# Softcap attention and a maxout MoE block on one core: the fourth quad's softmax sums from VectorE additions and four products

## The chip, the cores and the metric

One core of a Trainium2 chip runs the whole program. The metric is the device time of one execution in microseconds, as the median of several executions. A profile belongs to one execution of its own; its span leaves out a little at the start and the end.

A core has five engines that run at the same time, each through its own list of instructions: TensorE (PE; its weight loads are PEld), VectorE (DVE), ScalarE (ACT), GpSimd (POOL) and SyncE (SP, which here only issues DMAs). An engine works through its list in order; it waits where an instruction needs what another engine or a DMA has not delivered yet.

## The reference

Attention with a soft cap on the scores, and then a block with two input matrices whose larger result is taken:

```python
scores = (q @ k.T) / sqrt(64)                  # 8 batches, 12 heads, 448 x 448
scores = cap * tanh(scores / cap)              # cap = 30
attn   = exp(scores - max(scores))
attn   = attn / (sum(attn, axis=-1) + 1e-9)
x      = (attn @ v)                            # 3584 tokens x 768
g      = maximum(x @ w1, x @ w2)               # 3584 x 1024
out    = g @ w_out                             # 3584 x 768
```

What matters here is the sum over the keys, one number for each query of each head.

## The kernel before

Heads are taken in pairs: eight batches of six pairs give 48 pairs, and two neighbouring pairs make a *quad*, so there are 24 quads, t = 0 to 23. Three pairs make a *group* for loading (g = 0 to 15).

The scores are computed transposed: keys on partitions, queries along the row. A head's 448 keys are three chunks of 128 (j = 0 to 2) and a rest of 64. `scores(t, p)` forms the products of pair p of quad t (p = 2 holds the rests of both pairs), and ScalarE takes the tanh out of PSUM at once (L319). `ex` then takes the exponential (L324) into the tiles `expo[t, 0]`, `expo[t, 1]` and `expo[t, 2]`, in bfloat16. No maximum is subtracted.

Since keys lie on partitions, their sum is a product with a matrix of ones. `total(t)` (L352) does it for the four heads of a quad in four column strips of 32, in one PSUM bank. It has two forms. For t < NS it takes each chunk by itself: three chunks and the rest for four heads, sixteen products (L358, L362). For other quads VectorE has added the chunks elementwise beforehand into the tile `esum[t]`, and `total` needs one product for each head, four in all (L365). The additions are made by `add(t, ab, step)` (L331), which returns at once for t < NS: step 0 adds chunks 0 and 1 of pair ab (L344), step 1 adds chunk 2 (L346), step 2 adds the rest, which fills 64 partitions (L342). Two pairs and three steps make six additions for a quad.

After the sums, VectorE turns them (L367), takes reciprocals (L369) and turns them back (L371); `values(t)` forms the products with v (L381, L387), and `normalize` multiplies (L402), which writes x.

The MoE block of a batch, `moe(b)`, needs x of three quads. Its work is *fill*: a generator whose single products are handed out by `F(n)`, so many between other instructions. Its first layer makes eight groups of six products (L414) of x with `wd_sb`, which holds the difference of the two input matrices; each group is emptied from PSUM by VectorE with a relu (L419). Then come the output products (L429 with x, L432 with g), emptied by L435. The PSUM banks for all of these, `mm`, come from a pool of two, so a group can start only when the group two before it has been emptied.

The order of everything is written out by hand. There is a prologue for quads 0 to 2, and a loop over t from 3 to 23, in which the scores of quad t+1 are formed while the sums and values of quad t are finished. In the loop the calls of `add` for quad t are strewn between fills: after 6 and 2 products `add(t,0,0)`, after 3 more `add(t,0,1)`, after 3 `add(t,1,0)`, then 2, the scores of the next quad, 3, `add(t,1,1)`, 7, `add(t,0,2)`, 4, `add(t,1,2)`, 8, the rest scores, `total(t)` and `values(t)`. In the turn t = 3 one subtraction for the weights, `subtract(5, 1, nc.vector)` (L236), stands ahead of `add(t,0,1)`.

Keys and queries of groups from 2 on are loaded in float32 by SP, cast to bfloat16 by GpSimd (L185, L190, L197) into `kqf`, and transposed by a DMA that SP issues (`cross`, L292) into `qkT`, from which the scores are formed. Values are cast by GpSimd too (L164, L169). During the turn t = 3 GpSimd makes the last subtraction of the weights that falls to it, casts keys and queries of the end of group 3, and then casts values.

Of the kernel before, what the change touches and what calls it, by code (L numbers as in the profile page):

```python
# [10 lines left out]
def kernel(  # L11
# [287 lines left out]
    def two_banks(pool):  # L299
        return pool.tile([P, 2, 512], f32, name="s" if pool is s_psum else "v")  # L300
# [30 lines left out]
    def add(t, ab, step):  # L331

        if t < NS or t >= NQ:
            return
# [17 lines left out]
    def total(t):  # L352

        ss = two_banks(s_psum)[:, 0, :]
        if t < NS:
            for j in range(NJ):
# [117 lines left out]


    NL = N // L
    NS = 4
    todo = [[] for _ in range(N)]
    crosses = {}
    casts = [[] for _ in range(NQ)]  # L480
# [247 lines left out]
```

## Time and profile before

| quantity | value |
|---|---|
| median of 5 executions | 340.42 us (339.79 to 341.38) |
| the profiled execution | 340.82 us, of which its span is 338.8 us |
| granted TensorE clock | 1.00 |
| sixteen products of a sum (L358, L362), quad 3 | start 63.02 us, next work starts 63.78 us |
| four products of a sum (L365), quad 4 | start 75.22 us, next work starts 75.42 us |
| an addition into esum (L344, L346, L342) | 0.61 us at the least, 0.96 and 1.45 at the most for L344 and L346 |
| eviction of a group of the first layer (L419) | 0.62 us |
| DMA bytes moved | 61.78 MB, mean 182 GB/s |

Times in the profile count from the start of the span. A line of an order of time gives the start, the length, the engine, the line of the kernel, the operation, what it writes and reads with the shapes, how many such instructions are merged, and in brackets the idle time before it with what ended it.

### The profile page before, as it was taken

The page shows a single profiled execution, that of the slowest core. Times are in us where ns is not written, and L with a number is a line of the kernel's source. Part 1 is how long each engine was busy: PE and PEld are TensorE (multiplying, and loading weights), DVE is VectorE, ACT ScalarE, POOL GpSimd, SP SyncE. Part 2 cuts the span into 40 slices and gives each one's busy share as a digit, 9 for nine tenths or more (in the row PEclk, how much of TensorE's full clock was granted, in tenths as well). Part 3 has the DMA queues.
Part 4 walks back from the last instruction along what each step waited for, and adds up shares of the span by engine and source line. Part 5 has one row for each costly group of instructions (what it writes and reads, how often), then busy time and mean ns, then how long its engine had stood idle before and what let it go on. Part 6 is the DMA issues. An engine that isn't in the chain of part 4 may idle for free.

```text
span 338.8 us, 6879 instructions
## 1 busy us (share of the span) xinstructions
PE 324.5 (96%) x2722; PEld 163.7 (48%) x2722; DVE 229.7 (68%) x414; ACT 278.5 (82%) x243; POOL 112.6 (33%) x196
## 2 busy tenths in 40 slices
PE   3799999999899999999999999999999999999995
PEld 2455544455345454455445544545444554555562
DVE  4546866687787776767777668775876777874421
ACT  4999989999999999899989999999989999800000
POOL 8335687554224422431440442144034220000000
PEclk9999999999999999999999999999999999999999
DMA  7999999999996699558958599749955920012032
GB/s 218 192 234 268 275 261 273 268 240 259 206 301 148 186 228 269 143 141 206 303 124 198 75 250 316 170 121 236 304 104 133 221 94 2 0 48 93 2 93 93
DMA packets 106239, 61.78 MB, mean 182 GB/s; under 512 B 62816, under 2 KB 101216, under 8 KB 106208
## 3 DMA queue, kind: packets, MB, share of 16 engines
q1 hardware_dynamic: 102336, 58.21, 67.2%
q0 software_dynamic: 3872, 3.15, 6.0%
q8 instruction: 21, 0.34, 0.5%
q14 instruction: 10, 0.08, 0.1%
HBM read 42.47 MB, written 11.01 MB: 158 GB/s over the span
## 4 chain that ended last, share of the span: by engine, by line
PE 80%; DMA 9%; POOL 4%; DVE 4%; SPq 1%; issue 1%; POOLq 0%; DVEq 0%
PE mm L432 22%; PE mm L414 18%; PE mm L429 16%; PE v L381 6%; PE s L318 6%; DMA gT<-in_moe_w_dram 3%; PE mm L256 2%; PE v L318 2%; DMA osb<-in_moe_w_dram 2%; PE s L315 2%; PE v L387 2%; PE s L365 2%; DMA qkT<-kqf 2%; POOL wd_sb L236 2%; DMA vr<-in_v_dram 1%
## 5 line engine op out<-in xcount | busy, mean ns | idle before, releaser
L324 ACT ACTIVATE expo<-tanh 128x2688 bf16<-128x2688 bf16 (+1 forms) x72 | 140.3, 1950 | 0.2
L319 ACT ACTIVATE tanh<-s 128x896 bf16<-128x896 f32 x123 | 107.5, 915 | 14.1 <-PE s L318 10.6
L432 PE MATMUL mm<-wo_sb,gT 128*128 128x384 bf16 x448 | 85.8, 327 | 0.0
L414 PE MATMUL mm<-xT,wd_sb 128*128 128x448 bf16 x384 | 78.1, 353 | 0.9 <-DVE gT L419 0.7
L429 PE MATMUL mm<-wm_sb,xT 128*128 128x384 bf16 x336 | 66.1, 327 | 0.0
L435 DVE COPY osb<-mm 128x384 f32<-128x384 f32 x56 | 31.1, 556 | 44.5 <-PE mm L432 44.0
L432 PEld LDWEIGHTS <-gT 128*128 128x128 bf16 x448 | 42.3, 98 | 34.4 <-issue 8.2
L414 PEld LDWEIGHTS <-wd_sb 128*128 128x128 bf16 x384 | 35.9, 98 | 39.1 <-issue 8.5
L419 DVE TENSOR_SCALAR gT<-mm 128x448 bf16<-128x448 f32 x64 | 39.5, 622 | 19.8 <-PE mm L414 19.6
L688 POOL COPY mark<-inv 1x1 f32<-1x1 f32 x17 | 3.0, 178 | 125.3 <-DVE inv L371 109.7
L429 PEld LDWEIGHTS <-xT 128*128 128x128 bf16 x336 | 31.6, 98 | 26.4 <-issue 6.7
L319 ACT ACTIVATE tanh<-v 128x896 bf16<-128x896 f32 x45 | 41.5, 923 | 0.0
L381 PE MATMUL v<-expo,vp 128*32 128x448 bf16 x576 | 36.0, 353 | 0.0
L318 PE MATMUL s<-qkT 64*128 64x448 bf16 x198 | 28.5, 363 | 1.9 <-DVE qkT L288 1.5
L402 DVE TENSOR_TENSOR xT<-v,inv 128x448 bf16<-128x448 f32 x48 | 27.7, 620 | 2.6 <-PE v L387 0.3
L346 DVE TENSOR_TENSOR esum<-esum,expo 128x896 bf16<-128x896 bf16 x40 | 27.4, 686 | 0.8
L367 DVE STREAM_TRANSPOSE st<-s 128x448 f32<-128x448 f32 x24 | 15.6, 650 | 17.0 <-PE s L365 12.7
L344 DVE TENSOR_TENSOR esum<-expo 128x896 bf16<-128x896 bf16 x40 | 26.6, 666 | 0.0
L342 DVE TENSOR_TENSOR esum<-esum,expo 64x896 bf16<-64x896 bf16 x40 | 24.7, 617 | 1.2
L318 PEld LDWEIGHTS <-qkT 64*128 64x128 bf16 x288 | 10.5, 95 | 24.4 <-issue 16.9
L381 PEld LDWEIGHTS <-vp 128*32 128x32 bf16 x576 | 15.6, 97 | 10.2 <-DVE vl L161 0.4
L185 POOL CAST kqf<-qr 128x1152 bf16<-128x1152 f32 (+2 forms) x17 | 17.1, 1003 | 7.4 <-DMA qr<-in_q_dram 6.5
(68 smaller groups left out, 265.5 us busy)
## 6 DMA issues: line engine op xcount, KB each, us to landing
vr<-in_v_dram SPq DMA_DIRECT2D x14, 576.0 KB, 5.0
out_dram<-osb SPq DMA_DIRECT2D x20, 384.0 KB, 3.6
kr<-in_k_dram SPq DMA_DIRECT2D x12, 576.0 KB, 6.7
qr<-in_q_dram SPq DMA_DIRECT2D x12, 576.0 KB, 7.1
out_dram<-osb SPq DMA_DIRECT2D x16, 192.0 KB, 4.3
osb<-in_moe_w_dram SPq DMA_DIRECT2D x8, 256.0 KB, 4.8
gT<-in_moe_w_dram POOLq DMA_DIRECT2D x12, 128.0 KB, 9.4
wo_sb<-in_moe_w_out_dram POOLq DMA_DIRECT2D x4, 384.0 KB, 9.2
```

Of the source, the lines that this page charges most:

```text
L318: nc.tensor.matmul(s[:, m, :S], k0[r, j * P : (j + 1) * P], qTn[r, :])
L319: nc.scalar.activation(tanh[t, p][:, 2 * j : 2 * j + 2, :], s[:, :, :S], AF.Tanh, scale=scale / cap)
L324: nc.scalar.activation(expo[t, p], tanh[t, p][:, 0:n, :], AF.Exp, scale=float(cap))
L344: nc.vector.tensor_add(d, e_of(t, ab, 0), e_of(t, ab, 1))
L346: nc.vector.tensor_add(d, d, e_of(t, ab, 2))
L381: nc.tensor.matmul(ps[r, :S], vp[g % 2][:, 2 * n + h, j, u::2], e_of(t, ab, j)[:, h, :], start=(j == 0), stop=False,)
L402: nc.vector.tensor_mul(x_of(t, u), ps[:, u, :S], inv[t])
L414: nc.tensor.matmul(ps[:, :S], wd_sb[:, c, f * P : (f + 1) * P], x[:, c, cs], start=(c == 0), stop=(c == KC - 1))
L419: nc.vector.tensor_relu(g[f // FH][:, f % FH, cs], ps[:, :S])
L429: nc.tensor.matmul(ps[:, : DM // 2], x[:, c, ts], wm_sb[:, c, hs], start=(c == 0), stop=False)
L432: nc.tensor.matmul(ps[:, : DM // 2], g[f // FH][:, f % FH, ts], wo_sb[:, f, hs], start=False, stop=(f == FC - 1))
L435: nc.vector.tensor_copy(osb[:, hs], ps[:, : DM // 2])
```

## The change

One constant changes. `NS` is read in `add` and in `total` and nowhere else, so quad 3, the first of the loop, moves from the first form of the sum to the second: its six calls of `add` now issue additions, and its `total` issues four products from `esum[3]` instead of sixteen from the `expo` tiles. Quads 0 to 2 keep the sixteen products; quads 4 to 23 had the additions already.

```diff
     NL = N // L
-    NS = 4
+    NS = 3
     todo = [[] for _ in range(N)]
```

The lines that read it, in `add` (L333) and in `total` (L355):

```python
        if t < NS or t >= NQ:
            return
...
        if t < NS:
            for j in range(NJ):
...
        else:
            for ab, h, r in HEADS:
                nc.tensor.matmul(ss[r, :S], ones[:, :32], esum[t][:, 2 * ab + h, :], start=True, stop=True)
```

## The prediction

> **What bounds the kernel now.** I read the page's busy shares first, then the chain of waits, then the order of time around the one place that the change can touch. NS is read only in `add` (L333) and `total` (L355), so going from 4 to 3 alters quad t=3 and nothing else. Which products are t=3's? There are 48 on L358, twelve for each of four quads, and the last twelve start at 63.02 us; so the place is the loop's first turn, about 53.5 to 67 us.
>
> ```profile
> PE 324.5 (96%) x2722; PEld 163.7 (48%) x2722; DVE 229.7 (68%) x414; ACT 278.5 (82%) x243; POOL 112.6 (33%) x196
> ...
> PE 80%; DMA 9%; POOL 4%; DVE 4%; SPq 1%; issue 1%; POOLq 0%; DVEq 0%
> ```
>
> TensorE is the bound: it carries 80% of the chain, and it works through its list in a fixed order. A stall that it takes in the middle isn't won back, because no later part of it waits for slack. From 54.9 to 66.0 us (table of stages) PE is busy 10.85 of 11.10 us, ACT 11.01, POOL 8.48, DVE 7.22. VectorE seems to have 3.9 us free. The question is whether that free time lies where the additions land. TensorE in order of time (start, length, engine, line, what it writes and reads, how many):
>
> ```profile
> 57.28 0.55 PE L318 MATMUL s<-qkT 64*128 64x448 bf16 x4
> 58.07 0.36 PE L318 MATMUL v<-qkT 64*128 64x448 bf16 x2 [0.25 <-ACT tanh L319]
> 58.37 4.34 PE L414 MATMUL mm<-xT,wd_sb 128*128 128x448 bf16 x22
> 62.54 0.54 PE L315 MATMUL s<-qkT 128*128 128x448 bf16 x2
> 63.02 0.75 PE L358 MATMUL s<-expo,ones 128*32 128x448 bf16 x12
> 63.59 0.36 PE L362 MATMUL s<-expo,ones 128*32 128x448 bf16 x4
> 63.78 0.74 PE L381 MATMUL v<-expo,vp 128*32 128x448 bf16 x12
> ```
>
> Ahead of these stand 16 more products of L414, from 54.14. They and the 22 are fill, the first layer of the first MoE block: groups of six into one PSUM bank, two banks in turn (the pool `mm` has two). So group n+2 may start only when VectorE has emptied group n (L419). VectorE, GpSimd and SP's queue in the same stretch:
>
> ```profile
> 55.87 0.62 DVE L419 TENSOR_SCALAR gT<-mm 128x448 bf16<-128x448 f32 x1 [0.51 <-PE mm L414]
> 56.41 1.37 DVE L236 TENSOR_TENSOR wd_sb<-xT,gT 128x512 bf16<-128x512 f32 x1
> 57.70 0.61 DVE L419 TENSOR_SCALAR gT<-mm 128x448 bf16<-128x448 f32 x1
> ```
> ```profile
> 58.05 0.82 POOL L185 CAST kqf<-kr 128x768 bf16<-128x768 f32 x1 [0.82 <-DMA kr<-in_k_dram]
> 58.82 0.64 POOL L197 CAST kqf<-kr 64x128 bf16<-64x128 f32 x2
> 59.52 0.83 POOL L185 CAST kqf<-qr 128x768 bf16<-128x768 f32 x1
> 60.42 0.40 POOL L190 CAST kqf<-qr 64x256 bf16<-64x256 f32 x1
> ```
> ```profile
> 60.84 3.02 SPq L292 DMA_TRANSPOSE qkT<-kqf  x1
> ```
>
> See three things: the subtraction of L236 took 1.37 us on DVE while GpSimd ran its own from 56.08 to 57.23 (the other two on DVE took 0.76 and 0.68); GpSimd is casting from 58.05 to 60.82; and the moment its last cast ends, 60.82, SP issues the transposing DMA at 60.84. That one lands for the scores at 67.11, where the chain has a DMA piece of 6.22 us.
>
> **What the Trainium skill says.** "SBUF — State Buffer", section "SBUF: two separate sides": a VectorE operation with two SBUF inputs and a GpSimd operation that reads SBUF share a port pair, which is an exclusive lock held for the whole instruction; who starts first has it and the other blocks. "GPSIMD Engine Reference", section "Specifications", lists the same contention. The trace agrees, in the next quad's additions:
>
> ```profile
> 69.93 1.45 DVE L346 TENSOR_TENSOR esum<-esum,expo 128x896 bf16<-128x896 bf16 x1
> ```
> ```profile
> 69.68 1.22 POOL L185 CAST kqf<-qr 128x1152 bf16<-128x1152 f32 x1 [4.26 <-DMA qr<-in_q_dram]
> 70.86 0.89 POOL L190 CAST kqf<-qr 64x384 bf16<-64x384 f32 x1
> ```
>
> An addition alone takes 0.61; this one ends at 71.38, 0.48 after the cast's end at 70.90 (the subtraction above: 0.55 after GpSimd's). The cast behind it takes 0.89 where it takes 0.51 alone, and ends 0.37 after the addition, its own length less 0.14. I use both rules below. "TensorEngine Tiling (Array Packing)", section "Tiling Modes": 128x32 tiles work independently, four at once. The trace agrees: twelve products of 353 ns start within 0.57 us, 0.19 for four. So the removed products are cheap.
>
> **The change part by part.** Removed on TensorE: sixteen products run from 63.02 to the first of `values` at 63.78, 0.76 us; the four that replace them took 0.20 in quad 4 (75.22 to 75.42). Saved: 0.56 us, on the path. Added on VectorE: six additions, 6 x 0.61 = 3.7 us without contention, queued in program order among the evictions. I follow them, counting products of the layer: ten ran before 53.5, the 16 of 54.14 are numbers 11 to 26, the 22 are 27 to 48, 0.19 us apart; an eviction follows numbers 12, 18, 24 and so on.
>
> 1. Up to the eviction of group 3 (55.87 to 56.49) nothing changes. The first addition (head pair 0) stands where the subtraction stood, behind GpSimd's L236, which ends at 57.23: it ends at 57.71.
> 2. The subtraction follows: 57.63 to 58.31, in time for product 30 at 58.94.
> 3. GpSimd's cast of 58.05 gets the lock next and ends at 58.31 + 0.68 = 58.99; the second addition ends at 59.47.
> 4. Only then the eviction of group 4: 59.40 to 60.02 instead of 57.70 to 58.31. Group 6 starts with product 31, due at 58.37 + 4 x 0.19 = 59.13. It waits to about 60.1: **stall 0.95 us**.
> 5. Additions three and four stand ahead of the eviction of group 5. The third, 59.95 to 60.56 if it beats the next cast; that cast ends at 61.25, the fourth addition at 61.73; eviction 61.66 to 62.28. Group 7, due at 60.1 + 6 x 0.19 = 61.27, waits to 62.35: **stall 1.08 us**.
> 6. The eviction of group 6 ends at 62.9, before product 43 is due at 63.5: no stall. The last two additions end about 64.3, with some contention from the casts of v; `total` is reached about 65.1. No stall, slack 0.8.
>
> TensorE's own sum: +0.95 +1.08 -0.56 = +1.47 us. At 67.11 the scores wait for the transposing DMA now, which hides part: the last fill product starts at 66.72, and after fills of the same kind the scores follow 0.25 later, so TensorE would have been ready at 66.97 and 0.14 of the delay is covered. The transposition itself: its last cast ends at 61.73 + 0.26 = 61.99 instead of 60.82, so it lands 1.17 later. TensorE at 66.97 + 1.47 = 68.44 comes after 67.07 + 1.17 = 68.24, so the evictions decide. **Net +1.3 us.** Behind the moved DMA, SP's loads of q and v of the next groups slip 1.17 too; their transposition was issued at 71.77 and, with the same 6.2 us, lands at 78.0, the scores that need it start at 78.79; both slip, the cover stays. ScalarE had no gap from 49.7 to 67.04, but its next inputs come later as well, and it idles instead: later stages have it busy 10.8 to 11.7 of 11 to 12.5 us, so it catches up.
>
> The profiled execution took 340.82 us (span 338.8 and 2.0 around it); it becomes 342.1. It lies 0.4 above the median 340.42; on the median the forecast is 341.7.
>
> Bounds. Nothing in the trace shows additions, a subtraction and this many casts together. Least: VectorE wins each lock after the first; the evictions of groups 4 and 5 end at 59.39 and 60.99, stalls 0.3 and 0.4, net +0.2 or below. That needs GpSimd to lose where at 69.68 it won. Most: GpSimd wins the race at step 5 too, +0.3, and each of the last additions waits for a cast so that `total` stalls 0.5: about +2.1. I take +1.3.
>
> **Rivals.**
> Additions hidden (not slower). For it: in turn t=6 the same six additions stand among the same evictions, and the products (16 from 91.13, 22 from 94.93) run on, with 0.15 us at most between two weight loads:
>
> ```profile
> 93.58 1.10 DVE L346 TENSOR_TENSOR esum<-esum,expo 128x896 bf16<-128x896 bf16 x1
> 94.61 0.76 DVE L344 TENSOR_TENSOR esum<-expo 128x896 bf16<-128x896 bf16 x1
> 95.29 0.61 DVE L419 TENSOR_SCALAR gT<-mm 128x448 bf16<-128x448 f32 x1
> ```
>
> That eviction ended at 95.90, just as its bank was due (94.93 + 5 x 0.19 = 95.88). Against it: t=6 has no subtraction, fewer casts, and one lock wait fewer. This decides if the eviction of group 4 ends before 59.1 and that of 5 before 60.3. Then 0.14 to 0.56 us is won: 339.9 to 340.3.
>
> The transposition takes over. If every cast from 58.05 waits for an addition and the last for two, SP issues about 2.3 us later: the scores stand at 69.4, net +2.3, 342.7. Against it: VectorE spends part of that time in evictions, which read PSUM.
>
> A later stall goes. At 85.3 to 86.3 TensorE waits 0.6 to 1.0 us for an addition behind an output copy; if the slip reorders these, the loss is cancelled or, with hidden additions, 339.2 results. Nothing points to the order changing, as both engines slip together.
>
> That the change doesn't do what it says I exclude: both places that read NS switch together.
>
> **How the numbers follow.** About 0.3%, 1.0 us, can be told from no change. Forecast 0.62 (0.55 beyond 1.0 us, 0.07 inside); hidden 0.18 (0.14 inside, 0.04 faster); transposition 0.13, all slower; later stall 0.07 (0.04 faster, 0.03 inside). Sums: faster 0.08, same 0.24, slower 0.68. Range 340.0 to 343.3: it takes most of the hidden case and the transposition's; the forecast's own is 340.6 to 342.5.
>
> **What would show it.** In the profile after: gaps between the products of the first layer around 59 to 62.5 us with VectorE's eviction as releaser; evictions of groups 4 and 5 near 60.0 and 62.2; additions of 0.9 to 1.4 us beside GpSimd's casts; SP's transposition at about 62.0; `total` about 2 us later and 0.56 shorter. The forecast is wrong if the 22 products still run without a gap, or if the scores at 67 start no later than now.

## The result and the profile after

The median went from 340.58 us (80 runs) to 341.56 us (43 runs). The ratio is 1.0026, with a 95% interval of 1.0018 to 1.0035: 0.6 to 1.2 us slower. The profiled execution took 341.79 us, with a span of 339.9 us. The page's shares of busy time and its chain by engine hardly moved:

```profile
PE 324.0 (95%) x2710; PEld 163.3 (48%) x2710; DVE 234.0 (69%) x420; ACT 278.4 (82%) x243; POOL 114.0 (34%) x196
...
PE 82%; DVE 6%; DMA 5%; ACT 3%; POOL 1%; issue 1%; DVEq 0%; POOLq 0%; ACTq 0%
```

TensorE has twelve instructions fewer, VectorE six more and 4.3 us more busy time (waits inside an instruction count as busy), and TensorE still bounds. The change is visible only in the order of time. TensorE in the turn of quad 3, after:

```profile
52.78 0.55 PE L318 MATMUL s<-qkT 64*128 64x448 bf16 x4
...
57.68 0.93 PE L414 MATMUL mm<-xT,wd_sb 128*128 128x448 bf16 x4
59.64 1.30 PE L414 MATMUL mm<-xT,wd_sb 128*128 128x448 bf16 x6 [1.03 <-DVE gT L419]
61.87 2.43 PE L414 MATMUL mm<-xT,wd_sb 128*128 128x448 bf16 x12 [0.93 <-DVE gT L419]
64.14 0.54 PE L315 MATMUL s<-qkT 128*128 128x448 bf16 x2
64.61 0.37 PE L365 MATMUL s<-esum,ones 128*32 128x448 bf16 x4
64.81 0.74 PE L381 MATMUL v<-expo,vp 128*32 128x448 bf16 x12
...
68.00 0.55 PE L318 MATMUL s<-qkT 64*128 64x448 bf16 x4
```

Where 22 fill products ran without a gap there are now two gaps, each ended by an eviction, the VectorE instruction (L419) that empties a PSUM bank. VectorE and GpSimd in the same stretch:

```profile
55.18 0.62 DVE L419 TENSOR_SCALAR gT<-mm 128x448 bf16<-128x448 f32 x1 [0.51 <-PE mm L414]
55.72 0.62 DVE L344 TENSOR_TENSOR esum<-expo 128x896 bf16<-128x896 bf16 x1
56.25 1.64 DVE L236 TENSOR_TENSOR wd_sb<-xT,gT 128x512 bf16<-128x512 f32 x1
57.82 1.24 DVE L346 TENSOR_TENSOR esum<-esum,expo 128x896 bf16<-128x896 bf16 x1
58.98 0.61 DVE L419 TENSOR_SCALAR gT<-mm 128x448 bf16<-128x448 f32 x1
59.51 0.61 DVE L344 TENSOR_TENSOR esum<-expo 128x896 bf16<-128x896 bf16 x1
60.16 1.13 DVE L346 TENSOR_TENSOR esum<-esum,expo 128x896 bf16<-128x896 bf16 x1
61.21 1.14 DVE L419 TENSOR_SCALAR gT<-mm 128x448 bf16<-128x448 f32 x2
```
```profile
55.78 1.57 POOL L236 TENSOR_TENSOR wd_sb<-xT,gT 128x512 bf16<-128x512 f32 x1
57.30 1.28 POOL L185 CAST kqf<-kr 128x768 bf16<-128x768 f32 x1
58.53 1.04 POOL L197 CAST kqf<-kr 64x128 bf16<-64x128 f32 x2
59.63 1.19 POOL L185 CAST kqf<-qr 128x768 bf16<-128x768 f32 x1
60.88 0.67 POOL L190 CAST kqf<-qr 64x256 bf16<-64x256 f32 x1
```

VectorE has no idle time from 55.18 to 65.69. The work alone doesn't fill it: the subtraction took 1.64 us instead of 0.68, two additions 1.24 and 1.13 instead of 0.61. GpSimd's instructions beside them are longer too (1.57 instead of 1.15, 1.28 and 1.19 instead of 0.83, 0.67 instead of 0.40). Each waits for the other's, as the prediction had read it from the next quad's additions.

To leave start-up differences out (the prologue, equal in both kernels, ended 0.69 us earlier in this execution), I use one measure below, the *stretch*: from the first product of quad 4's scores to that of quad 5's. It was 67.11 - 53.47 = 13.64 us before and is 68.00 - 52.78 = 15.22 us. The two ends before:

```profile
53.47 0.55 PE L318 MATMUL s<-qkT 64*128 64x448 bf16 x4
...
67.11 0.55 PE L318 MATMUL s<-qkT 64*128 64x448 bf16 x4
```

### The profile page after: what moved, and what is told of

Same layout as the page of the kernel before. It is cut to its first block, busy times and chain, and to the rows that moved or that the text cites. A ratio compares the mean times of both kernels' runs of the same rounds, so it can differ in the third digit from the quotient of the medians.

```text
span 339.9 us, 6861 instructions
## 1 busy us (share of the span) xinstructions
PE 324.0 (95%) x2710; PEld 163.3 (48%) x2710; DVE 234.0 (69%) x420; ACT 278.4 (82%) x243; POOL 114.0 (34%) x196
## 3 DMA queue, kind: packets, MB, share of 16 engines
q1 hardware_dynamic: 102336, 58.21, 66.9%
## 4 chain that ended last, share of the span: by engine, by line
PE 82%; DVE 6%; DMA 5%; ACT 3%; POOL 1%; issue 1%; DVEq 0%; POOLq 0%; ACTq 0%
PE mm L432 22%; PE mm L414 18%; PE mm L429 17%; PE v L381 7%; PE s L318 6%; DMA wo_sb<-in_moe_w_out_dram 5%; PE s L315 2%; PE v L387 2%; PE v L318 2%; PE mm L256 2%; PE s L365 2%; ACT tanh L319 2%; ACT expo L324 2%; DVE gT L419 1%; DVE esum L344 1%
## 5 line engine op out<-in xcount | busy, mean ns | idle before, releaser
L419 DVE TENSOR_SCALAR gT<-mm 128x448 bf16<-128x448 f32 x64 | 39.3, 622 | 17.3 <-PE mm L414 17.0
L346 DVE TENSOR_TENSOR esum<-esum,expo 128x896 bf16<-128x896 bf16 x42 | 28.5, 678 | 0.8
L344 DVE TENSOR_TENSOR esum<-expo 128x896 bf16<-128x896 bf16 x42 | 28.3, 674 | 0.0
L342 DVE TENSOR_TENSOR esum<-esum,expo 64x896 bf16<-64x896 bf16 x42 | 26.3, 626 | 1.3
```

The costliest lines, as they stand in the source:

```text
L344: nc.vector.tensor_add(d, e_of(t, ab, 0), e_of(t, ab, 1))
L346: nc.vector.tensor_add(d, d, e_of(t, ab, 2))
L419: nc.vector.tensor_relu(g[f // FH][:, f % FH, cs], ps[:, :S])
```

## The experiments

Theory: evictions queue behind additions that wait for GpSimd, and the fill waits for the evictions. Rivals: VectorE's own time is the cost; the transposing DMA, late behind GpSimd's casts, is the cost; the products removed count for nothing. Line numbers are those of each run's own kernel, so in some the products and evictions stand one or three lines further on.

**The changed kernel again** (`again`, no edit).

> The changed kernel once more, as a second profile. All theories: ratio to the kernel before 1.002 to 1.0035. As a measure that start-up jitter does not touch, I take the stretch from the first product of the first scores of quad 4 to that of quad 5: 13.64 us before, 15.22 us after in the profiles so far; here 15.0 to 15.4. If the stretch varied by more than 0.3 us between executions, the local reading would be worth little.

Ratio 1.0031 (1.0013 to 1.0049). The stretch was 69.01 - 53.18 = 15.83 us, outside what I expected. The instructions are the same, but GpSimd's subtraction came at another moment and caught the first addition as well:

```profile
56.12 1.23 DVE L344 TENSOR_TENSOR esum<-expo 128x896 bf16<-128x896 bf16 x1
57.27 1.64 DVE L236 TENSOR_TENSOR wd_sb<-xT,gT 128x512 bf16<-128x512 f32 x1
58.83 1.24 DVE L346 TENSOR_TENSOR esum<-esum,expo 128x896 bf16<-128x896 bf16 x1
```

One addition 0.61 us longer, and the stretch 0.61 us longer. By the limit that I had set (0.3 us), one profile's stretch is worth little as a size. Below I use it to see which wait does what, and the medians for what it costs.

**Additions alone** (`adds_only`).

```diff
-        if t < NS:
+        if t <= NS:
             for j in range(NJ):
```

> Quad 3's six additions are made, but its total still takes the sixteen products. Theory (evictions queue behind the additions, and the products removed were on TensorE's path): 0.56 us more than the changed kernel, stretch 15.8 us, ratio 1.0042. Rival (TensorE had slack at the sum, so the products are worth nothing): as the changed kernel, 15.2 us, 1.0026.

Ratio 1.0030 (1.0013 to 1.0046), between the two expectations, and it separates nothing. In this profile GpSimd met fewer of the additions: the evictions of groups 4 and 5 start at 58.21 and 60.03, the stretch is 14.66 us.

**The same VectorE time with one SBUF input** (`turns_only`).

```diff
+        if t == NS:
+            nc.vector.transpose(att.tile([P, S], f32, name="dummy", bufs=1), inv[2])
+            return
         if t not in esum:
...
-        if t < NS:
+        if t <= NS:
             for j in range(NJ):
```

> Quad 3's total takes the sixteen products; at the places of the six additions VectorE makes six 32x32 transpositions of an old 128x448 fp32 tile into a scratch tile (0.65 us each, one SBUF input, results unused): the same VectorE time as the additions, with one SBUF input instead of two. Theory (half of the loss is the wait for GpSimd at the shared port): evictions of groups 4 and 5 end at about 58.9 and 60.6, one stall of about 0.35 us, stretch 13.9 us, ratio 1.0006. Rival (VectorE's plain time is the cost, whatever the operation): as with the additions and sixteen products, stretch 15.6 to 15.8 us, ratio 1.0042.

Ratio 1.0003 (0.9989 to 1.0017), stretch 66.38 - 52.69 = 13.69 us. VectorE was given 6 x 0.65 = 3.9 us, more than the additions' 3.7, and the 22 products ran on (4.53 us, 4.34 before). Three of the transpositions and GpSimd's casts of keys and queries lie over each other, and none is longer than alone:

```profile
56.76 0.64 DVE L336 STREAM_TRANSPOSE dummy<-inv 128x448 f32<-128x448 f32 x1
57.31 0.59 DVE L422 TENSOR_SCALAR gT<-mm 128x448 bf16<-128x448 f32 x1
57.82 1.30 DVE L336 STREAM_TRANSPOSE dummy<-inv 128x448 f32<-128x448 f32 x2
```
```profile
57.12 0.82 POOL L185 CAST kqf<-kr 128x768 bf16<-128x768 f32 x1 [0.99 <-PE s L318]
57.89 0.64 POOL L197 CAST kqf<-kr 64x128 bf16<-64x128 f32 x2
58.59 0.83 POOL L185 CAST kqf<-qr 128x768 bf16<-128x768 f32 x1
```

One thing in this profile is chance: GpSimd's last subtraction had ended at 56.13, just ahead of VectorE's at 56.19, which so ran unhindered. The medians don't hang on one profile: against `adds_only`, which differs only in what VectorE does for quad 3, they are 340.82 and 341.69 us, and resampling the 22 times of each gives 0.5 to 1.4 us for the difference. VectorE's own time is not the cost; that rival falls.

**Products alone** (`products_only`).

```diff
-        if t < NS or t >= NQ:
+        if t <= NS or t >= NQ:
             return
...
-                nc.tensor.matmul(ss[r, :S], ones[:, :32], esum[t][:, 2 * ab + h, :], start=True, stop=True)
+                e = e_of(t, ab, 0)[:, h, :] if t == NS else esum[t][:, 2 * ab + h, :]
+                nc.tensor.matmul(ss[r, :S], ones[:, :32], e, start=True, stop=True)
```

> No additions for quad 3, and its total takes four products of the first chunk alone; the other chunks and the rests of the keys are left out of quad 3's sums. Theory (the transposition issued when GpSimd's last cast ends is late next and caps the gain at 0.14 us): stretch 13.5 us, ratio 0.9996. Rival (the saving counts in full): stretch 13.1 us, ratio 0.9984.

Ratio 0.9995 (0.9977 to 1.0014), stretch 14.25 us. Neither size came, and the place of the wait did:

```profile
65.23 0.65 PE L433 MATMUL mm<-wo_sb,gT 128*128 128x384 bf16 x3
67.13 0.55 PE L318 MATMUL s<-qkT 64*128 64x448 bf16 x4 [1.25 <-DMA qkT<-kqf]
```

Without a stall ahead of it TensorE reaches the scores early and stands 1.25 us for the transposing DMA, which can't come before the keys and queries. In an execution in which that data is late, the saving is hidden.

**Without VectorE's subtraction** (`no_sub`).

```diff
+    nc.vector.memset(wd_sb[:, 5:6, DF // 2 :], 0.0)
...
         if t == 3:
-            subtract(5, 1, nc.vector)
+            pass
```

> The changed kernel without VectorE's subtraction for the weights in the turn of quad 3; that sixth of the second half of the weight difference is left out (zeros, set at the start). Theory (evictions late behind additions and subtraction that wait at the shared port): the eviction of group 4 comes about 1.2 us earlier and no longer stalls, group 5 stalls 0.2 to 0.4 us, and the transposing DMA, still late behind additions, sets the next scores: stretch 14.0 to 14.4 us (15.22 and 15.83 in the two profiles of the changed kernel), ratio 1.001. Rival (the additions' own time is the cost): 15 us, 1.003.

Ratio 1.0010 (0.9995 to 1.0025), as expected; the stretch is 65.73 - 52.45 = 13.28 us, shorter than expected. All six additions are there and the 22 products run on (4.57 us). The rival's 1.003 lies outside the interval. The stretch alone doesn't show what the subtraction cost: in this profile GpSimd's last subtraction had ended at 55.24, before the first addition began at 55.38, so the short stretch isn't the work of the edit alone. The transposing DMA was issued 4.84 us before the scores, and no wait for it is shown:

```profile
60.89 1.80 SPq L292 DMA_TRANSPOSE qkT<-kqf  x1
```

It landed 4.7 us after its issue, so the 6.2 us of the kernel before are not a fixed length. In the profile after it took 4.3 us from its issue at 61.58: it had landed about 2.1 us before the scores at 68.00. A late transposition isn't what lengthens the stretch.

**Without GpSimd's subtractions** (`pool_clear`, on the changed kernel, and its base `pool_clear_base`, on the kernel before).

```diff
+    nc.vector.memset(wd_sb[:, 0:5, DF // 2 :], 0.0)
...
-    for c in range(5):
-        subtract(c, 1, nc.gpsimd)
```

> The changed kernel without GpSimd's five subtractions for the second half of the weights, which end just as the first addition is issued; that part of the weight difference is left out (zeros, set at the start). To be read against its own base, pool_clear_base. Theory (the loss depends on how GpSimd's subtractions and casts fall among the additions): the first addition and the subtraction wait no more, the eviction of group 4 is in time, group 5 stalls about 0.45 us; stretch 13.9 to 14.2 us, and 0.0 to 0.5 us over its base. Rival (GpSimd's phase has no part): 0.9 to 1.6 us over its base, as with the change itself.

> The kernel before without the same five subtractions of GpSimd, as the base for pool_clear; the same part of the weight difference is left out. Both theories: stretch 13.3 to 13.7 us, ratio 0.999 to 1.0005.

Ratios 1.0003 (0.9988 to 1.0018) and 0.9999 (0.9977 to 1.0021), stretches 13.29 and 13.50 us. VectorE makes all its additions and its subtraction, GpSimd makes all its casts, and no loss is seen: 340.28 us against the base's 340.47, and in the stretch 0.21 below the base, where 0 to 0.5 above was expected. With 14 executions each, a loss of some tenths of a us could hide in these medians. The instructions ahead of the eviction of group 4 have their plain length:

```profile
55.90 0.61 DVE L344 TENSOR_TENSOR esum<-expo 128x896 bf16<-128x896 bf16 x1
56.43 0.69 DVE L236 TENSOR_TENSOR wd_sb<-xT,gT 128x512 bf16<-128x512 f32 x1
57.03 0.62 DVE L346 TENSOR_TENSOR esum<-esum,expo 128x896 bf16<-128x896 bf16 x1
```

**Evictions first** (`evict_first`).

```diff
-        add(t, 0, 1)
+        else:
+            add(t, 0, 1)
         F(3)
-        add(t, 1, 0)
+        if t != 3:
+            add(t, 1, 0)
...
-        add(t, 1, 1)
-        F(7)
-        add(t, 0, 2)
-        F(4)
-        add(t, 1, 2)
-        extra(i + 1)
-        F(8)
+        if t == 3:
+            add(t, 0, 1)
+            F(1)
+            add(t, 1, 0)
+            F(6)
+            add(t, 1, 1)
+            F(4)
+            extra(i + 1)
+            F(2)
+            add(t, 0, 2)
+            F(6)
+            add(t, 1, 2)
...
+            x3 = values(t)
+            total(t)
+            normalize(t, x3)
```

> The changed kernel with quad 3's second to sixth addition moved, each behind the next eviction (of groups 4 to 8), and quad 3's values formed ahead of its total. Nothing is left out. Theory (evictions late behind additions stall the fill): the 22 products run without a gap, and the next late thing shows: the transposing DMA behind GpSimd's casts, delayed by the additions, or the total behind the last addition; stretch 14.3 to 14.7 us, ratio 1.0012 to 1.002. Rival (the fill's stalls only take the place of the late transposition, so removing them gains nothing): stretch 15.2 us or more, ratio 1.0026.

Ratio 1.0042 (1.0024 to 1.0061), no better than the change (1.0026; the intervals overlap). The fill did run without a gap, and the stretch is 14.00 us, but the loss now lies beyond its end. The sums now end so late that the PSUM tile of the values is free late, and the third part of the same scores waits for it:

```profile
57.80 4.43 PE L414 MATMUL mm<-xT,wd_sb 128*128 128x448 bf16 x22
...
66.89 0.55 PE L318 MATMUL s<-qkT 64*128 64x448 bf16 x4
68.26 0.37 PE L318 MATMUL v<-qkT 64*128 64x448 bf16 x2 [0.82 <-DVE xT L402]
```

I had named the transposition and the total as next late; it was the normalization. The order cures the stall it was made for and pays elsewhere.

**The kernel before again** (`before_again`, no edit of the kernel before).

> The kernel before once more, as a second profile of it and as a measure of what two copies of one kernel differ by. All theories: ratio 0.9985 to 1.0015; stretch 13.4 to 14.3 us, the upper end where GpSimd's casts come late and the scores wait for the transposing DMA.

Ratio 1.0003 (0.9988 to 1.0017). The stretch was 67.47 - 52.70 = 14.77 us: 1.13 more than in the first profile of the same kernel. Here GpSimd's weights had come late (it waited 2.8 us for them), and TensorE waits for GpSimd's last subtraction and twice for a transposition:

```profile
56.88 0.55 PE L318 MATMUL s<-qkT 64*128 64x448 bf16 x4 [0.31 <-DMA qkT<-kqf]
...
58.87 3.96 PE L414 MATMUL mm<-xT,wd_sb 128*128 128x448 bf16 x20 [0.72 <-POOL wd_sb L236]
...
67.47 0.55 PE L318 MATMUL s<-qkT 64*128 64x448 bf16 x4 [0.31 <-DMA qkT<-kqf]
```

So the kernel before loses time in this stretch too in some executions, which may be why the medians differ by less than the first two profiles.

**GpSimd later** (`pool_late`, on the changed kernel, and `pool_late_base`, on the kernel before).

```diff
+        if c == 4:
+            nc.gpsimd.memset(att.tile([P, 768], f32, name="idle", bufs=1), 0.0)
         subtract(c, 1, nc.gpsimd)
```

> The changed kernel with one more GpSimd instruction (a fill of a scratch tile with zeros, about 0.73 us, unused) ahead of GpSimd's last subtraction in the turn of quad 3. To be read against its own base, pool_late_base. Theory (the loss is set by how far GpSimd's reads push the additions, and with them the evictions): the first addition, the subtraction and all behind them end about 0.7 us later, the fill waits about 0.7 us more; stretch 15.9 to 16.5 us, ratio 1.004 to 1.005, and 1.2 to 2.2 us over the base. Rival (the phase of GpSimd has no part, the loss is VectorE's own time): the same 0.9 us over the base as the change, or less.

> The kernel before with the same GpSimd instruction, as the base for pool_late. Both theories: VectorE has room for its one late subtraction, so only the casts and the transposing DMA come later; stretch 13.6 to 14.3 us, ratio 1.000 to 1.002.

Ratios 1.0027 (1.0015 to 1.0038) and 1.0007 (0.9994 to 1.0020), stretches 14.76 and 13.98 us. The expected growth did not come; by the ratios the cost is that of the change. The profile shows a fault in the experiment: the fill with zeros made a gap in GpSimd's reads, in which the first addition ended and the subtraction ran unhindered. It changed which instructions meet GpSimd's reads, instead of only delaying them. So this run doesn't test what it was made for.

```profile
55.74 1.18 DVE L344 TENSOR_TENSOR esum<-expo 128x896 bf16<-128x896 bf16 x1
56.85 0.68 DVE L236 TENSOR_TENSOR wd_sb<-xT,gT 128x512 bf16<-128x512 f32 x1
57.45 1.57 DVE L346 TENSOR_TENSOR esum<-esum,expo 128x896 bf16<-128x896 bf16 x1
```
```profile
56.38 0.74 POOL L607 MEMSET idle<- 128x768 f32 x1
57.08 1.46 POOL L236 TENSOR_TENSOR wd_sb<-xT,gT 128x512 bf16<-128x512 f32 x1
```

**The subtraction given to GpSimd** (`sub_pool`).

```diff
-    for c in range(5):
+    for c in range(6):
         subtract(c, 1, nc.gpsimd)
...
         if t == 3:
-            subtract(5, 1, nc.vector)
+            pass
```

> The changed kernel with VectorE's subtraction of the turn of quad 3 given to GpSimd, as the sixth of its row; nothing is left out. It tests a rule read from five profiles: the stretch is 13.1 us plus the time by which the additions and the subtraction that stand ahead of the eviction of group 5 exceed their own 0.61 and 0.68 us (2.11 us gave 15.22, 2.73 gave 15.83, 1.63 gave 14.76; 0.97 gave 14.66, of which 0.56 are the twelve more products of that kernel). Rule: stretch within 0.2 us of 13.1 plus the excess, where the excess is over 0.2 us and TensorE does not wait for GpSimd's subtraction or the transposing DMA. I expect an excess of 0.5 to 1.2 us, since one wait fewer can arise, stretch 13.6 to 14.3 us, ratio 1.000 to 1.002. Rival (VectorE's own time counts, and 0.68 us of it are gone, but GpSimd's casts come 1.15 us later): the transposing DMA is waited for, stretch 14.5 us or more, ratio 1.0025.

Stretch 66.60 - 52.80 = 13.80 us, in the expected span, but my rule fails: the additions ahead of group 5's eviction exceeded their own time by 1.18 us, which would give 14.28. The rule counted the waits and forgot that the subtraction's own 0.68 us had left the queue. Ratio 1.0038 (1.0016 to 1.0061), above what I expected; the rival's wait for the transposition isn't there. From the end of the stretch to quad 8's first scores (turns 4 to 6) this profile loses another 0.8 us against the first profile of the kernel before. A stretch alone is therefore not the whole bill. From its start to quad 8's first scores it is 49.58 and 50.95 us in the two profiles of the kernel before, 51.42 and 51.53 in those of the changed kernel, 50.53 in `sub_pool`, 50.82 in `evict_first`, and 49.69 in `turns_only` and `pool_clear`.

What holds in all profiles where VectorE was given work for quad 3 (but `evict_first`, which exchanges sum and values) is simpler. I set the end of group 5's eviction (its start plus 0.62), counted from the start of the stretch, beside the length of the stretch; 0.56 is taken off where the sum has sixteen products:

| kernel | eviction of group 5 ends | stretch | difference |
|---|---|---|---|
| `again` | 9.66 | 15.83 | 6.17 |
| after | 9.05 | 15.22 | 6.17 |
| `pool_late` | 8.57 | 14.76 | 6.19 |
| `adds_only` | 7.92 | 14.66 - 0.56 = 14.10 | 6.18 |
| `sub_pool` | 7.62 | 13.80 | 6.18 |
| `pool_clear` | 7.05 | 13.29 | 6.24 |
| `turns_only` | 6.98 | 13.69 - 0.56 = 13.13 | 6.15 |
| `no_sub` | 6.98 | 13.28 | 6.30 |

Over 2.7 us of range the stretch follows that one eviction to within 0.1 us: behind it TensorE runs on to the next scores without a gap. The relation was found after the runs, and none was made to test it.

## Why the prediction was right

The forecast was 341.7 us, 1.3 over the median; measured are 341.56 us and 1.0 over it. The mechanism was right: evictions late behind VectorE instructions that wait for GpSimd. Which instruction waits, and so the size, depends on the execution. Its steps, with the profile after moved by its 0.69 us of earlier start:

- *The bound and the place* (TensorE, quad 3's turn): right. The gaps are in the 22 products, ended by evictions.
- *Saved 0.56 us*: right in the profile: four products and the next work are 0.20 us apart, 64.61 to 64.81. In the medians it can't be seen: `adds_only` and `again` have 341.69 and 341.74 us. `products_only` shows that other data can hide it.
- *Steps 1 and 2*: the waiting instruction was another. The first addition came ahead of GpSimd's subtraction and ended at 56.34 (57.03 in the earlier count, 57.71 foretold); GpSimd's subtraction, held by it, ended at 57.35 (58.04; foretold 57.23); VectorE's took the wait instead and ended at 57.89 (58.58; foretold 58.31). In `again` both wait.
- *Steps 3 and 4*: eviction of group 4 foretold to end at 60.02, measured 59.59 + 0.69 = 60.28. The product was due at 57.68 + 4 x 0.19 = 58.44 and started at 59.64: a stall of 1.20 us, 0.95 foretold.
- *Step 5*: foretold 62.28 and 1.08 us (by its own numbers the product was due at 61.24, not 61.27); measured 61.83 + 0.69 = 62.52, and 61.87 - (59.64 + 6 x 0.19) = 1.09 us.
- *Step 6*: right; the last twelve products and the total have no gap.
- *The cover of 0.14 us*: right. From the first output product to the scores it took 67.11 - 65.40 = 1.71 us before and 68.00 - 66.43 = 1.57 now.
- *The transposition 1.17 us later*: its issue was nearly right (61.58 + 0.69 = 62.27, foretold 62.0), its length wrong. It was costed with the same 6.2 us and took 4.3. So the evictions decided by about 2.1 us, not by the 0.2 foretold.
- *Net*: 1.20 + 1.09 - 0.56 - 0.14 = 1.59, the measured 15.22 - 13.64 = 1.58; foretold 1.3. The term most too small was the first stall, by 0.25 us.
- *From the profile to the median*: the sum was made against one execution of the kernel before, in which only the cover of 0.14 us was lost there. `before_again` shows another that loses 1.13 us more in the same stretch. This is a likely reason that the medians part by 1.0 and not 1.6 us; a distribution of stretches over unprofiled runs wasn't measured. That 1.3 lies so near 1.0 is in part luck: from one profile to another the change is anything from 15.22 - 14.77 = 0.45 to 15.83 - 13.64 = 2.19 us.

The rival of hidden additions rested on turn t=6, where nothing stalled. In the profile after, the same mechanism strikes there too, since GpSimd's cast of v (92.98 to 94.13) now runs when the first addition is issued:

```profile
93.21 1.40 DVE L344 TENSOR_TENSOR esum<-expo 128x896 bf16<-128x896 bf16 x1
94.53 0.61 DVE L419 TENSOR_SCALAR gT<-mm 128x448 bf16<-128x448 f32 x1
```
```profile
91.89 3.01 PE L414 MATMUL mm<-xT,wd_sb 128*128 128x448 bf16 x15
95.19 0.35 PE L414 MATMUL mm<-xT,wd_sb 128*128 128x448 bf16 x1 [0.29 <-DVE gT L419]
```

The eviction is late, one product waits 0.29 us. In `again` the cast of v came later (94.58), and the same turn took as long as before. So t=6 showed one order of instructions, and no evidence of room. The rival of the transposition is refuted as the cause of the stretch, as it had landed in time; that a later stall would go isn't seen: the 0.63 us wait for L342 ahead of quad 5's total is in both profiles.

Open: what the changed kernels lose in turns 4 to 6. In the profiles after, of `adds_only`, `pool_late`, `no_sub`, `pool_clear` and `sub_pool` it is 0.26 to 0.8 us more than in the first profile of the kernel before, in `again` 0.2 less; but `before_again`, without the change, has 0.24 more as well. Only the wait above is traced. Open too is why `sub_pool`, with a short stretch, has a median 0.7 us over the kernel before.

No version here beats the kernel before: the best that the products can give is 0.56 us, 0.16%, less than the width of any interval here.

## What to carry to other kernels

Before work is moved to an engine with free time, look at what stands behind it in that engine's queue and when that is due: here 3.7 us of additions into 3.9 us of apparent room cost about 1 us, because GpSimd's reads held them up and PSUM evictions stood behind them. Count for VectorE instructions with two SBUF inputs not their own length but the length beside GpSimd's work: `turns_only` gave VectorE even more to do, with one SBUF input, and cost nothing measurable. And take two profiles before a sum is made against one: the same kernel's stretch was 13.64 and 14.77 us.

## What the runs showed of the hardware

The Trainium skill, "SBUF — State Buffer", section "SBUF: two separate sides", says that against a VectorE operation with two SBUF inputs only those GpSimd operations count that read SBUF. `pool_late` agrees: the first addition ended at 56.92 and the subtraction, with its plain 0.68 us, began at 56.85, both within the fill with zeros (56.38 to 57.12); in the profile after, the subtraction took 1.64 us beside GpSimd's subtraction. An fp32 transposition of 128x448 on VectorE (0.65 us) was not held by GpSimd's casts either, in `turns_only`. The transposing DMA of SP at the end of quad 3's turn was occupied 2.88 to 3.06 us in its issue in the six profiles in which quad 3 has no additions, and 1.78 to 1.88 us in the eight in which it has. It is not a matter of when it was issued: 8.86 us after the start of the stretch in `before_again` (2.88 us), 8.80 in the profile after (1.79). From issue to landing it took 4.3 to 5.1 us in the eight and 4.6 to 6.3 in the six; why wasn't tried.
